# A gated attention decode kernel: the gate sum moved into the third projection's transposition, one signal for each query parity, the output sum copied in halves, the w2 products split

## The chip, the cores and the metric

The kernel runs on 1 core of one Trainium2 chip. The time is the device time of one execution in microseconds (us). A core has five engines that run programs of their own and meet at semaphores: TensorE (PE, matrix products), VectorE (DVE), ScalarE (ACT), GpSimd (POOL) and SyncE (SP, which here only issues DMAs).

## The reference

Two sequences, one token each, model width 448, 16 heads of 256, a cache of 4096 keys and values, and a dense block of 1792. All is float32.

```python
g = sigmoid((x * gate_w).sum(-1, keepdims=True))
q = (x @ wq).reshape(2, 1, 16, 256).transpose(0, 2, 1, 3)
p = softmax(einsum("bhqd,bhkd->bhqk", q, k_cache) * 256 ** -0.5)
a = einsum("bhqk,bhkd->bhqd", p, v_cache).reshape(2, 1, 4096) @ wo
b = relu(x @ w1) @ w2
out = g * a + (1 - g) * b
```

## The kernel before, in words

**The stream.** Every input is read once. There are U = 32 units, one for each pair of sequence and head. Row `kv[u]` (8 MB) holds the values of unit u and the keys of unit u+1. It lands in one of two slots of the ring in SBUF, `slot[u % 2]`. SP issues all large transfers in one hand-written order (L110 to L135): the two halves of wq, `kv[0]`, the keys of unit 0, the values of unit 1, w1, the keys of unit 2 (second half of `kv[1]`), then `kv[2]` to `kv[30]`, the values of unit 31, w2, and wo in six pieces of 13, 11, 4, 2, 1 and 1 chunks, the last ones the smallest. A transfer into a slot waits for `free`, which VectorE raises when it is done with the unit that lay there.

**A unit.** ScalarE copies the unit's query column out of `qt` into `query` (`pick`, L278). TensorE computes its scores with 16 matmuls (32 recorded passes, L192) into the one PSUM tile `ps`. VectorE takes the negative maximum (`peak`, L312), ScalarE the exponential with its sum (`exponents`, L283), and VectorE multiplies the 8 value blocks by the probabilities (`value`, L316). VectorE takes the next unit's maximum after its sixth value block. So while VectorE works on the values of u, TensorE does the scores of u+1. On ScalarE the order is: wait for the maximum, exponential, then `arrive` (L273: wait for the landing of `kv[u]`, raise `vals`), then `pick` of u+1, whose keys landed with it. VectorE waits for `prob` and `vals` before the values of u.

**The head.** POOL forms `gs`, the products of x and gate_w summed down to one number per partition; TensorE adds them over the partitions with a matmul of ones (L170), and ScalarE takes both sigmoids from it (L259, L260) and zeroes the PSUM tile `az` (L261). Then two projections with wq (L179), each copied to `wide` by ScalarE, transposed (L183) and copied to `qt`. The third projection, x @ w1, is done by TensorE once w1 has landed; ScalarE handles it in a branch in the middle of the loop, in its first turn after the second exponential (L292 to L302).

**The tail.** When w2 has landed, TensorE adds the 14 w2 chunks (28 passes, L226) into `acc`. After the last value block VectorE and ScalarE rescale the four partial softmaxes (L334 to L341), with two TensorE steps between (L231 into `wp`, L235 into `po`), and VectorE writes the gated attention output to `lhs` (L345, signal `ot`). Then TensorE adds 30 wo chunks (60 passes, L226), chunk groups as they land. The last two chunks go straight into `z` (L250). ScalarE copies `acc` to SBUF (L308), TensorE folds its four parts into `z` (L253), VectorE copies the result (L349), and SP writes it out.

**The branch hint.** TensorE's program is laid out in blocks. A never-taken branch at L244 back to the block `tail` carries a hint that is set at the very start (L168).

Of the kernel before, what the change touches and what calls it, by code (L numbers as in the profile page):

```python
# [9 lines left out]
G = 4  # L10
# [6 lines left out]
def take(e, sem, n=1):  # L17
    e.wait_ge(sem, n)
    e.sem_inc(sem, -n)  # L19
# [7 lines left out]
def gated_mix_decode(nc, xg, kv, wq, w1, w2, wo, out):  # L27
# [20 lines left out]
    NQ = H * DH // (G * CW)  # L48
    FG = NF * P // G
    WQ = wq.shape[2]  # L50
    SCALE = float(DH) ** -0.5
    assert NQ == 2 and U % 2 == 0 and U > 4 and FG == D and BL * GAP == NE * D and w1.shape[1] == WQ == BL * CW

    def sbuf(name, *shape):
        return nc.alloc_sbuf_tensor(name, [*shape], F32).ap()
# [5 lines left out]
    for n in (13, 11, 4, 2, 1, 1):  # L61
        WO.append(WO[-1] + n)
    assert WO[-1] == N
    names = ["xg", "wq", "w2", *(f"wo{k}" for k in WO[2:]), *(f"land{s}" for s in range(SLOTS)), "early",
             "pool", "vec", "act", "xr", "sums", "gate", "omg", "proj", "spent", "wide", "pt", "relu", "hr",
             "query", "score", "top", "prob", "vals", "free", "tr", "nb", "e4", "wb", "wp", "os", "po", "ot",
             "acc", "a", "z", "res", "out"]
    sem = {n: nc.alloc_semaphore(n) for n in names}
    land = [sem[f"land{s}"] for s in range(SLOTS)]

# [5 lines left out]
    ident = sbuf("ident", P, P)  # L76
    ones = sbuf("ones", P, P)
    sel2 = sbuf("sel2", P, HP)
    sel4 = sbuf("sel4", P, G, R)
    sel = sel4[:, 0]  # L80
    pg = sbuf("pg", P, B, KC)
    gs = sbuf("gs", P, B)
    gate = sbuf("gate", P, B)
    omg = sbuf("omg", P, B)
# [19 lines left out]
    acc, z = az[:, :D], az[:, CW:CW + DG]  # L104
    mt, lp, wp, gp = tp[:U, 0:P:R], tp[U:2 * U, 0:P:R], tp[:, 2 * P:2 * P + U], tp[:, 3 * P:3 * P + B]

# [35 lines left out]
    def gpsimd(e):  # L142
        settle(e, sem["pool"], e.memset(ident, 0.0))
        settle(e, sem["pool"], e.affine_select(out=ident, in_=ident, compare_op=ALU.not_equal, fill=1.0, base=0,
                                               pattern=[[-1, P]], channel_multiplier=1))
        e.memset(ones, 1.0)
        e.memset(qt[:, :, U:], 0.0)
        e.wait_ge(sem["xg"], 16)
        settle(e, sem["pool"], e.tensor_tensor(pg, xg_sb[:, :, :B].rearrange("p c b -> p b c"),
                                               xg_sb[:, None, :, B].to_broadcast([P, B, KC]), op=ALU.mult))  # L150
        settle(e, sem["pool"], e.memset(pg[HP:, :, KF:], 0.0))
        settle(e, sem["pool"], e.tensor_tensor(pg[:, :, :KC // 2], pg[:, :, :KC // 2], pg[:, :, KC // 2:], op=ALU.add))
        e.tensor_tensor(gs, pg[:, :, 0], pg[:, :, 1], op=ALU.add).then_inc(sem["sums"], 1)  # L153
        e.tensor_copy(xr.rearrange("p c (b r) -> p c b r", b=B),
                      xg_sb[:, :, :B, None].to_broadcast([P, KC, B, RB])).then_inc(sem["xr"], 1)
        settle(e, sem["pool"], e.tensor_tensor(sel2, ident[:, :HP], ident[:, HP:], op=ALU.add))
        e.tensor_tensor(sel4, sel2[:, None, :R].to_broadcast([P, G, R]), sel2[:, None, R:].to_broadcast([P, G, R]),
                        op=ALU.add)
        e.wait_ge(sem["omg"], 1)
        e.wait_ge(sem["relu"], 1)  # L160
        hid = lhs[:, :NF]
        settle(e, sem["pool"], e.tensor_tensor(hid, hid, omg[:, None, :].to_broadcast([P, NF, B]), op=ALU.mult))
        e.wait_ge(sem["w2"], 16)
        e.sem_inc(sem["hr"], 1)  # L164

    def tensor(e):
        outer = nc.cur_bb.parent
        stay = e.mark_branch_hint_location()  # L168
        e.wait_ge(sem["sums"], 1)
        e.matmul(gp, ones, gs, start=True, stop=True).then_inc(sem["gate"], 1)  # L170
        e.wait_ge(sem["xr"], 1)
# [13 lines left out]

        def scores(keys):
            take(e, sem["query"])
            for c in range(SG // CW):
                for t in range(T):
                    for g in range(G):  # L190
                        at = t * S + g * SG + c * CW
                        m = e.matmul(ps[g * R:(g + 1) * R, c * CW:(c + 1) * CW],  # L192
                                     query[:, t:t + 1].to_broadcast([P, R]), keys[:, at:at + CW], start=t == 0,
                                     stop=t == T - 1)
                        if c == SG // CW - 1 and t == T - 1:
                            m.then_inc(sem["score"], 1)
# [8 lines left out]
        for s in range(SLOTS):  # L205
            scores(slot[1 - s][:, VL:])
        e.br("next")
# [5 lines left out]
        nc.switch_bb("rest", parent=outer)  # L213
        e.wait_ge(sem["query"], 1)
        e.transpose(tp[:2 * U, :P], nl, ident).then_inc(sem["tr"], 1)  # L215
# [11 lines left out]

        for k in range(NF):
            add(k)
        e.wait_ge(sem["wb"], 1)  # L230
        e.transpose(wp, wb.rearrange("u g r -> u (g r)"), ident[:U, :U]).then_inc(sem["wp"], 1)  # L231
        e.br("tail")
        nc.switch_bb("tail", parent=outer)
        e.wait_ge(sem["os"], 1)
        e.matmul(po[:, :G * nu], sel4.rearrange("p g r -> p (g r)"), os.rearrange("p u j -> p (u j)"), start=True,  # L235
                 stop=True).then_inc(sem["po"], 1)
        for k in range(NF, N - DIRECT):
            if k == NF:
                e.wait_ge(sem["ot"], 17)
            elif k in WO:  # L240
                e.wait_ge(sem[f"wo{WO[WO.index(k) + 1]}"], 16)
            m = add(k)
        m.then_inc(sem["acc"], 1)
        e.br_lt(turn, 0, on_true="tail", on_false="fold").branch_hint(stay)  # L244
        nc.switch_bb("fold", parent=outer)
        for k in range(N - DIRECT, N):
            e.wait_ge(sem[f"wo{k + 1}"], 16)
            for g in range(G):
                lo = (k - NF) * D + g * DG
                e.matmul(z[g * R:g * R + B], lhs[:, k], slot[0][:, lo:lo + DG], start=k == N - DIRECT, stop=False)  # L250
        e.wait_ge(sem["a"], 1)
        for g in range(G):
            m = e.matmul(z[g * R:g * R + B], sel[:, :B], a_sb[:, g * DG:(g + 1) * DG], start=False, stop=True)  # L253
        m.then_inc(sem["z"], 1)

    def scalar(e):
        bring(e, xg_sb, xg, sem["xg"])
        e.wait_ge(sem["gate"], 1)
        e.activation(omg, gp, AF.Sigmoid, scale=-1.0).then_inc(sem["omg"], 1)  # L259
        e.activation(gate, gp, AF.Sigmoid)  # L260
        e.activation(az, qt[:, 0, U:].to_broadcast([P, 2 * CW]), AF.Copy)  # L261
        for i in range(NQ):
# [7 lines left out]
                         pt.rearrange("p (s t n r) -> p s t n r", s=2, t=T, r=RB)[:, :, :, :, 0],  # L270
                         AF.Copy)

        def arrive(s):  # L273
            take(e, land[s], 16)
            e.sem_inc(sem["vals"], 1)

        def pick(u):
            e.activation(query, qt[:, :, bass.ds(u, 1)].rearrange("p t o -> p (t o)"), AF.Copy).then_inc(  # L278
                sem["query"], 1)

        def exponents(u, s):
            take(e, sem["top"])
            e.activation(prob[:, s * SG:(s + 1) * SG], ps, AF.Exp, bias=nm[:, bass.ds(u, 1)],  # L283
                         accum_out=ls[:, bass.ds(u, 1)]).then_inc(sem["prob"], 1)

        take(e, land[1], 16)
        pick(0)
        with e.Fori(0, U // 2) as i:
            for s in range(SLOTS):
                exponents(i * 2 + s, s)  # L290
                if s:
                    with e.If(i < 1):  # L292
                        take(e, sem["proj"])
                        e.activation(wide[:, :FG], ph[:, :FG], AF.Copy).then_inc(sem["wide"], 1)
                        take(e, sem["pt"])
                        e.activation(lhs[:, :G * KF],
                                     pt[:, :KF * P].rearrange("p (k b r) -> p k b r", b=B, r=RB)[:, :, :, 0], AF.Relu)
                        for h in range(2):
                            half = pt[:HP, KF * P + h * HP:KF * P + (h + 1) * HP]
                            m = e.activation(lhs[h * HP:(h + 1) * HP, G * KF:NF],  # L300
                                             half.rearrange("p (k b r) -> p k b r", b=B, r=RB)[:, :, :, 0], AF.Relu)
                        m.then_inc(sem["relu"], 1)  # L302
                arrive(s)
                pick(i * 2 + (s + 1))
        e.wait_ge(sem["nb"], 1)
        e.activation(e4, mt, AF.Exp, bias=nb, scale=-1.0).then_inc(sem["e4"], 1)
        e.wait_ge(sem["acc"], 1)
        e.activation(a_sb, acc, AF.Copy).then_inc(sem["a"], 1)  # L308

    def vector(e):  # L310
# [3 lines left out]
        def value(u, j, at, half):  # L314
            v = ring[:, bass.ds(at + j * SG, SG)]
            return e.scalar_tensor_tensor(v, v, 1.0, prob[:, bass.ds(half, SG)], op0=ALU.mult, op1=ALU.mult,  # L316
                                          accum_out=ov[:, bass.ds(u, 1), j])

        take(e, sem["score"], G)
        e.sem_inc(sem["free"], 1)  # L320
        peak(0)
        e.wait_ge(sem["early"], 16)
        with e.Fori(0, U) as u:
            take(e, sem["prob"])
            take(e, sem["vals"])
            for j in range(J):
# [87 lines left out]
```

## Time and profile before

| | |
|---|---|
| time, median of 3 runs | 675.07 us (674.78 to 675.76) |
| the profiled execution's own time | 674.93 us |
| its span, first to last instruction | 673.3 us |
| read from HBM | 289.54 MB |
| mean rate over the span | 430 GB/s |
| VectorE busy | 334.7 us (50%) |
| TensorE busy | 218.1 us (32%) |
| ScalarE busy | 71.4 us (11%) |

How to read it: the span lies 1.6 us under the time of the same execution; the rest is start and end around the first and last instruction. Timeline rows give start, duration, engine, line, operation, tile written and read, shape, and in brackets how long the engine had been idle and who released it. `x4` means four merged instructions, so the duration of a merged row covers all of them. A float32 matmul is recorded as two passes. PEld is the weight load of a matmul, PEclk the granted TensorE clock as a share of full.

### The profile page before, as it was taken

How to read it: one execution, taken by the hardware profiler on the slowest of the kernel's cores; microseconds unless marked ns; L12 is line 12 of the kernel's file. 1: busy time of each engine (PE TensorE's matmuls, PEld its weight loads, DVE VectorE, ACT ScalarE, POOL GpSimd, SP SyncE). 2: the span in 40 equal slices, each digit the busy share in tenths (PEclk: the TensorE clock that was granted, in tenths of full speed). 3: DMA queues.
4: the chain of work that ended last, by engine and by line, in shares of the span. 5: the costliest groups of instructions: out<-in, count | busy, mean ns of one | idle time of the engine just before them, and what ended most of it. 6: DMA issues, size and time to landing. Idle time of an engine off the chain costs nothing. (4 is left out here: it accounts for less than half of the span.)

```text
span 673.3 us, 4293 instructions
## 1 busy us (share of the span) xinstructions
PE 218.1 (32%) x1250; PEld 55.0 (8%) x1250; DVE 334.7 (50%) x556; ACT 71.4 (11%) x127; POOL 2.8 (0%) x16
## 2 busy tenths in 40 slices
PE   2146522233333212333331133333212333332247
PEld 0011100000000000000000000000000000000001
DVE  0005544566654445666444456654444666544491
ACT  1001110101001010101001010100101010010100
POOL 1000000000000000000000000000000000000000
PEclk9766766776765567676556767766556766655678
DMA  9999999999999999999999999999999999999997
GB/s 405 414 427 436 467 436 436 436 424 436 432 409 432 432 428 432 436 436 436 436 436 436 436 436 436 436 436 436 436 436 436 436 436 436 436 436 436 405 429 331
DMA packets 6625, 289.62 MB, mean 430 GB/s; under 512 B 992, under 2 KB 1248, under 8 KB 1504
## 3 DMA queue, kind: packets, MB, share of 16 engines
q1 hardware_dynamic: 6480, 289.60, 99.4%
q10 hardware_dynamic: 144, 0.01, 0.0%
q8 instruction: 1, 0.02, 0.0%
HBM read 289.54 MB, written 0.06 MB: 430 GB/s over the span
## 5 line engine op out<-in xcount | busy, mean ns | idle before, releaser
L316 DVE SCALAR_TENSOR_TENSOR ring<-ring,prob x256 | 297.9, 1220 | 269.8 <-DVEq L19 269.8
L192 PE MATMUL ps<-ring,query 128*32 128x512 f32 x1024 | 184.0, 884 | 405.2 <-PEq L19 405.2
L192 PEld LDWEIGHTS ps<-ring,query 128*32 128x32 f32 x1024 | 46.5, 154 | 541.4 <-issue 541.4
L312 DVE TENSOR_REDUCE nl<-ps 128x1024 f32 (+1 forms) x32 | 39.0, 1220 | 55.3 <-DVEq L19 55.3
L283 ACT ACTIVATE prob<-ps,nl 128x1024 f32<-128x1024 f32 x32 | 35.6, 1113 | 134.8 <-ACTq L19 134.6
L283 ACT ACT_TABLE_LOAD x16 | 20.5, 1283 | 132.9 <-ACTq L19 132.9
L278 ACT ACTIVATE query<-qt 128x2 f32 (+1 forms) x33 | 6.7, 204 | 262.9 <-ACTq L19 262.9
L179 PE MATMUL ph<-weights,xr 128*32 128x512 f32 (+1 forms) x96 | 15.0, 767 | 20.7 <-DMA weights<-in_wq 19.0
L316 DVE DVE_READ_ACCUMULATOR ring<-ring,prob x256 | 21.0, 82 | 0.0
L226 PE MATMUL az<-ring,lhs 128*2 128x448 f32 x60 | 8.8, 664 | 1.1 <-DVE lhs L345 1.0
L226 PE MATMUL az<-weights,lhs 128*2 128x448 f32 x28 | 5.7, 908 | 5.6 <-POOLq L164 5.6
L283 ACT ACTIVATION_READ_ACCUMULATOR prob<-ps,nl x32 | 6.2, 192 | 0.0
L179 PEld LDWEIGHTS ph<-weights,xr 128*32 128x32 f32 (+1 forms) x96 | 3.0, 133 | 31.2 <-DMA weights<-in_wq 19.2
L349 DVE COPY res<-az 128x112 f32<-128x112 f32 x1 | 0.3, 274 | 9.9 <-PE az L253 9.9
L170 PE MATMUL tp<-gs,ones 128*128 128x2 f32 x2 | 0.6, 364 | 13.3 <-POOL gs L153 13.3
L265 ACT ACTIVATE wide<-ph 128x512 f32<-128x512 f32 x2 | 1.2, 597 | 28.9 <-ACTq L19 28.9
L183 PE MATMUL pt<-ident,wide 128*128 128x128 f32 x12 | 2.0, 287 | 2.5 <-ACT wide L265 1.8
L226 PEld LDWEIGHTS az<-ring,lhs 128*2 128x2 f32 x60 | 1.8, 95 | 7.6 <-issue 4.1
L308 ACT ACTIVATE wide<-az 128x448 f32<-128x448 f32 x1 | 0.5, 543 | 12.6 <-PE az L226 12.6
L226 PEld LDWEIGHTS az<-weights,lhs 128*2 128x2 f32 x28 | 1.0, 114 | 9.4 <-POOLq L164 5.8
L183 PEld LDWEIGHTS pt<-ident,wide 128*128 128x128 f32 x12 | 1.3, 141 | 5.2 <-ACT wide L265 3.6
L215 PE MATMUL tp<-ident,nl 128*64 128x128 f32 x1 | 0.3, 299 | 4.3 <-ACT query L278 4.3
(43 smaller groups left out, 13.5 us busy)
## 6 DMA issues: line engine op xcount, KB each, us to landing
ring<-in_kv SPq DMA_DIRECT2D x4, 4096.0 KB, 24.8
weights<-in_wq SPq DMA_DIRECT2D x2, 3584.0 KB, 14.8
weights<-in_w SPq DMA_DIRECT2D x1, 3584.0 KB, 20.0
ring<-in_wo SPq DMA_DIRECT2D x1, 2912.0 KB, 12.0
weights<-in_w SPq DMA_DIRECT2D x1, 2688.0 KB, 23.9
ring<-in_wo SPq DMA_DIRECT2D x1, 2464.0 KB, 17.4
ring<-in_wo SPq DMA_DIRECT2D x1, 896.0 KB, 19.0
ring<-in_kv SPq DMA_DIRECT2D x30, 27.5
```

Of the source, the lines that this page charges most:

```text
L170: e.matmul(gp, ones, gs, start=True, stop=True).then_inc(sem["gate"], 1)
L179: m = e.matmul(ph[g * R:(g + 1) * R], xr[r, c], weights[r, at:at + CW], start=c == 0, stop=c == KC - 1)
L183: t = e.transpose(pt[:, k * P:(k + 1) * P], wide[:, k * P:(k + 1) * P], ident)
L192: m = e.matmul(ps[g * R:(g + 1) * R, c * CW:(c + 1) * CW], query[:, t:t + 1].to_broadcast([P, R]), keys[:, at:at + CW], start=t == 0, stop ...
L215: e.transpose(tp[:2 * U, :P], nl, ident).then_inc(sem["tr"], 1)
L226: return e.matmul(acc[g * R:g * R + B], lhs[:, k], w, start=k < G, stop=k >= N - DIRECT - G)
L265: e.activation(wide, ph, AF.Copy, scale=SCALE).then_inc(sem["wide"], 1)
L278: e.activation(query, qt[:, :, bass.ds(u, 1)].rearrange("p t o -> p (t o)"), AF.Copy).then_inc(sem["query"], 1)
L283: e.activation(prob[:, s * SG:(s + 1) * SG], ps, AF.Exp, bias=nm[:, bass.ds(u, 1)], accum_out=ls[:, bass.ds(u, 1)]).then_inc(sem["prob"], 1)
L308: e.activation(a_sb, acc, AF.Copy).then_inc(sem["a"], 1)
L312: e.tensor_reduce(nm[:, bass.ds(u, 1)], ps, axis=AX.X, op=ALU.max, negate=True).then_inc(sem["top"], 1)
L316: return e.scalar_tensor_tensor(v, v, 1.0, prob[:, bass.ds(half, SG)], op0=ALU.mult, op1=ALU.mult, accum_out=ov[:, bass.ds(u, 1), j])
```

## The change

- **Gate.** The matmul of ones, its two sigmoids and the `ones` tile go. POOL writes `gs`, repeated 32 times for each sequence, into the 64 columns of `wide` that the third projection leaves free (after both wq rounds: `spare`, then `column`). The third projection's transposition, which covered those columns already, turns them into rows; ScalarE copies these 64 rows with a sum over the free dimension (`gl`), POOL spreads the sums to the partitions with 8 small copies (`gp`), ScalarE takes one sigmoid in the branch of the first turn, and POOL forms 1 - gate.
- **Zeroing.** `az` is zeroed by VectorE at its start instead of by ScalarE.
- **Query signals.** `query` becomes `query0` and `query1`. TensorE only waits for one; ScalarE lowers it again before the exponential. TensorE's program loses two instructions by it.
- **Landing.** `arrive` and `vals` go. `exponents` now first waits for the landing of `kv[u]`, then for the maximum. VectorE waits for `prob` alone.
- **Tail.** The w2 products are split 8, 2 and 4 chunks: the step into `wp` comes after the first 8, the step into `po` after the next 2. The blocks `tail` and `fold` with their branches and the hint go. `acc` is copied in two halves of 224 columns, and each fold matmul waits for its half.

```diff
-        e.memset(ones, 1.0)
...
-        e.tensor_tensor(gs, pg[:, :, 0], pg[:, :, 1], op=ALU.add).then_inc(sem["sums"], 1)
+        settle(e, sem["pool"], e.tensor_tensor(gs, pg[:, :, 0], pg[:, :, 1], op=ALU.add))
...
-        e.wait_ge(sem["omg"], 1)
-        e.wait_ge(sem["relu"], 1)
+        e.wait_ge(sem["spare"], NQ)
+        e.tensor_copy(wide[:, FG:].rearrange("p (b r) -> p b r", b=B),
+                      gs[:, :, None].to_broadcast([P, B, R])).then_inc(sem["column"], 1)
+        e.wait_ge(sem["logit"], 1)
+        for g in range(G):
+            for b in range(B):
+                m = e.tensor_copy(gp[g * R:(g + 1) * R, b:b + 1], gl[HP + b * R:HP + (b + 1) * R, :1])
+        m.then_inc(sem["gate"], 1)
+        e.wait_ge(sem["sigmoid"], 1)
+        settle(e, sem["pool"], e.tensor_scalar(omg, gate, -1.0, 1.0, op0=ALU.mult, op1=ALU.add))
...
-        stay = e.mark_branch_hint_location()
-        e.wait_ge(sem["sums"], 1)
-        e.matmul(gp, ones, gs, start=True, stop=True).then_inc(sem["gate"], 1)
...
-        def scores(keys):
-            take(e, sem["query"])
+        def scores(s):
+            keys = slot[1 - s][:, VL:]
+            e.wait_ge(query_set[s], 1)
...
-        for k in range(NF):
+        for k in range(NF - 6):
             add(k)
         e.wait_ge(sem["wb"], 1)
         e.transpose(wp, wb.rearrange("u g r -> u (g r)"), ident[:U, :U]).then_inc(sem["wp"], 1)
-        e.br("tail")
-        nc.switch_bb("tail", parent=outer)
+        for k in range(NF - 6, NF - 4):
+            add(k)
         e.wait_ge(sem["os"], 1)
...
-        for k in range(NF, N - DIRECT):
+        for k in range(NF - 4, N - DIRECT):
...
-        e.br_lt(turn, 0, on_true="tail", on_false="fold").branch_hint(stay)
-        nc.switch_bb("fold", parent=outer)
...
-        e.wait_ge(sem["a"], 1)
         for g in range(G):
+            e.wait_ge(sem["a"], 1 + g * DG // HALF)
             m = e.matmul(z[g * R:g * R + B], sel[:, :B], a_sb[:, g * DG:(g + 1) * DG], start=False, stop=True)
...
-        e.wait_ge(sem["gate"], 1)
-        e.activation(omg, gp, AF.Sigmoid, scale=-1.0).then_inc(sem["omg"], 1)
-        e.activation(gate, gp, AF.Sigmoid)
-        e.activation(az, qt[:, 0, U:].to_broadcast([P, 2 * CW]), AF.Copy)
...
-        def arrive(s):
-            take(e, land[s], 16)
-            e.sem_inc(sem["vals"], 1)
...
         def exponents(u, s):
+            take(e, land[s], 16)
             take(e, sem["top"])
+            e.sem_inc(query_set[s], -1)
             e.activation(prob[:, s * SG:(s + 1) * SG], ps, AF.Exp, bias=nm[:, bass.ds(u, 1)],
                          accum_out=ls[:, bass.ds(u, 1)]).then_inc(sem["prob"], 1)
...
                     with e.If(i < 1):
                         take(e, sem["proj"])
+                        e.wait_ge(sem["column"], 1)
                         e.activation(wide[:, :FG], ph[:, :FG], AF.Copy).then_inc(sem["wide"], 1)
                         take(e, sem["pt"])
+                        e.activation(gl[HP:, 1:], pt[HP:, KF * P:], AF.Copy, accum_out=gl[HP:, :1]).then_inc(
+                            sem["logit"], 1)
...
-                        m.then_inc(sem["relu"], 1)
-                arrive(s)
-                pick(i * 2 + (s + 1))
+                        e.wait_ge(sem["gate"], 1)
+                        e.activation(gate, gp, AF.Sigmoid).then_inc(sem["sigmoid"], 1)
+                pick(i * 2 + (s + 1), 1 - s)
...
-        e.activation(a_sb, acc, AF.Copy).then_inc(sem["a"], 1)
+        for lo in range(0, D, HALF):
+            e.activation(a_sb[:, lo:lo + HALF], acc[:, lo:lo + HALF], AF.Copy).then_inc(sem["a"], 1)
...
+        e.memset(az, 0.0)
         take(e, sem["score"], G)
...
             take(e, sem["prob"])
-            take(e, sem["vals"])
```

More of the change, by code (lines that the diff above doesn't have):

```diff
@@ L49, in gated_mix_decode @@
     FG = NF * P // G
+    HALF = D // 2
     WQ = wq.shape[2]
@@ L64, in gated_mix_decode @@
     names = ["xg", "wq", "w2", *(f"wo{k}" for k in WO[2:]), *(f"land{s}" for s in range(SLOTS)), "early",
-             "pool", "vec", "act", "xr", "sums", "gate", "omg", "proj", "spent", "wide", "pt", "relu", "hr",
-             "query", "score", "top", "prob", "vals", "free", "tr", "nb", "e4", "wb", "wp", "os", "po", "ot",
+             "pool", "vec", "act", "xr", "spare", "column", "logit", "gate", "sigmoid", "proj", "spent", "wide", "pt", "hr",
+             "query0", "query1", "score", "top", "prob", "free", "tr", "nb", "e4", "wb", "wp", "os", "po", "ot",
              "acc", "a", "z", "res", "out"]
     sem = {n: nc.alloc_semaphore(n) for n in names}
+    query_set = [sem[f"query{s}"] for s in range(2)]
     land = [sem[f"land{s}"] for s in range(SLOTS)]
@@ L76, in gated_mix_decode @@
     ident = sbuf("ident", P, P)
-    ones = sbuf("ones", P, P)
     sel2 = sbuf("sel2", P, HP)
@@ L82, in gated_mix_decode @@
     gs = sbuf("gs", P, B)
+    gl = sbuf("gl", P, 1 + P)
+    gp = sbuf("gp", P, B)
     gate = sbuf("gate", P, B)
@@ L104, in gated_mix_decode @@
     acc, z = az[:, :D], az[:, CW:CW + DG]
-    mt, lp, wp, gp = tp[:U, 0:P:R], tp[U:2 * U, 0:P:R], tp[:, 2 * P:2 * P + U], tp[:, 3 * P:3 * P + B]
+    mt, lp, wp = tp[:U, 0:P:R], tp[U:2 * U, 0:P:R], tp[:, 2 * P:2 * P + U]
     def bring(e, dst, src, signal):
@@ L205, in tensor @@
         for s in range(SLOTS):
-            scores(slot[1 - s][:, VL:])
+            scores(s)
         e.br("next")
@@ L213, in tensor @@
         nc.switch_bb("rest", parent=outer)
-        e.wait_ge(sem["query"], 1)
+        e.wait_ge(query_set[0], 1)
         e.transpose(tp[:2 * U, :P], nl, ident).then_inc(sem["tr"], 1)
@@ L270, in scalar, with pick, exponents @@
                          pt.rearrange("p (s t n r) -> p s t n r", s=2, t=T, r=RB)[:, :, :, :, 0],
-                         AF.Copy)
-        def arrive(s):
-            take(e, land[s], 16)
-            e.sem_inc(sem["vals"], 1)
[L277 to L281, printed above, removed]
+                         AF.Copy).then_inc(sem["spare"], 1)
+        def pick(u, s):
+            e.activation(query, qt[:, :, bass.ds(u, 1)].rearrange("p t o -> p (t o)"), AF.Copy).then_inc(
+                query_set[s], 1)
+        def exponents(u, s):
+            take(e, land[s], 16)
             take(e, sem["top"])
+            e.sem_inc(query_set[s], -1)
             e.activation(prob[:, s * SG:(s + 1) * SG], ps, AF.Exp, bias=nm[:, bass.ds(u, 1)],
@@ L286, in scalar @@
         take(e, land[1], 16)
-        pick(0)
+        pick(0, 0)
         with e.Fori(0, U // 2) as i:
@@ L299, in scalar @@
                             half = pt[:HP, KF * P + h * HP:KF * P + (h + 1) * HP]
-                            m = e.activation(lhs[h * HP:(h + 1) * HP, G * KF:NF],
+                            e.activation(lhs[h * HP:(h + 1) * HP, G * KF:NF],
                                              half.rearrange("p (k b r) -> p k b r", b=B, r=RB)[:, :, :, 0], AF.Relu)
-                        m.then_inc(sem["relu"], 1)
-                arrive(s)
-                pick(i * 2 + (s + 1))
+                        e.wait_ge(sem["gate"], 1)
+                        e.activation(gate, gp, AF.Sigmoid).then_inc(sem["sigmoid"], 1)
+                pick(i * 2 + (s + 1), 1 - s)
         e.wait_ge(sem["nb"], 1)
```

## The prediction

> **What bounds the kernel now.** First the page: the span, the row of DMA shares, the instruction queue.
>
> ```profile
> span 673.3 us, 4293 instructions
> ...
> DMA  9999999999999999999999999999999999999997
> ...
> q8 instruction: 1, 0.02, 0.0%
> HBM read 289.54 MB, written 0.06 MB: 430 GB/s over the span
> ```
>
> The DMA engines are busy nine tenths or more in 39 of 40 slices, and 289.54 MB at 430 GB/s are the whole span. No engine can shorten that stream; it can only be interrupted, or the end behind its last byte can change. So I read the end next, in the chain that ended last.
>
> ```profile
> 650.65 19.90 DMA ring<-in_wo
> ...
> 670.60 0.37 PE az L250 x8
> 670.97 0.02 issue
> 670.99 0.42 PE az L253 x8
> ```
>
> The last wo piece lands at 670.55, and 2.7 us later the program ends. Two questions follow: does the changed kernel keep the queue full, and is everything but the last chunk done by 670.55? For both I read the timeline of the end.
>
> ```profile
> 637.64 0.20 ACT L278 ACTIVATE query<-qt 128x2 f32 x1 [8.23 <-ACTq L19]
> 637.91 1.22 DVE L316 SCALAR_TENSOR_TENSOR ring<-ring,prob  x1 [8.92 <-DVEq L19]
> ...
> 648.38 2.71 SPq L108 DMA_DIRECT2D ring<-in_wo  x6
> ...
> 653.48 5.66 PE L226 MATMUL az<-weights,lhs 128*2 128x448 f32 x28 [5.60 <-POOLq L164]
> ...
> 657.38 0.14 DVE L334 TENSOR_REDUCE nb<-tp 32x1 f32<-32x4 f32 x1
> ...
> 658.46 0.28 DVE L339 TENSOR_SCALAR wb<-e,rl 32x128 f32<-32x128 f32 x1
> ...
> 659.07 0.24 PE L231 MATMUL tp<-ident,wb 32*128 32x32 f32 x1
> ...
> 659.83 0.70 PE L235 MATMUL po<-os,sel 128*128 128x256 f32 x2 [0.51 <-DVE os L341]
> ...
> 661.54 8.81 PE L226 MATMUL az<-ring,lhs 128*2 128x448 f32 x60 [1.01 <-DVE lhs L345]
> ...
> 662.63 0.16 PEld L226 LDWEIGHTS az<-ring,lhs 128*2 128x2 f32 x4 [0.58 <-issue]
> 663.38 0.17 PEld L226 LDWEIGHTS az<-ring,lhs 128*2 128x2 f32 x4 [0.58 <-issue]
> ...
> 666.21 0.12 PEld L226 LDWEIGHTS az<-ring,lhs 128*2 128x2 f32 x8 [0.63 <-DMA ring<-in_wo]
> ...
> 669.43 0.09 PEld L226 LDWEIGHTS az<-ring,lhs 128*2 128x2 f32 x4 [0.86 <-DMA ring<-in_wo]
> ...
> 670.40 0.54 ACT L308 ACTIVATE wide<-az 128x448 f32<-128x448 f32 x1 [12.58 <-PE az L226]
> ```
>
> `kv[30]` has landed by 637.64. From 637.91 VectorE works without a gap to 657.4, then come the softmax steps, and TensorE starts the 60 wo passes at 661.54. It overtakes the stream: 0.63 us idle at 666.21, 0.86 at 669.43. So before the end there is slack, but little: the path from the landing of `kv[30]` through VectorE to TensorE is the second longest thing in the kernel. The stages show VectorE full and the clock that TensorE got:
>
> ```profile
> 646.00:653.40 7.40, 0.30 (x1) 0.11 (x1) 7.40 (x14) 1.30 (x3) 0.00 (x0) 0.65 1.00 429
> ...
> 658.50:661.90 3.40, 1.88 (x11) 0.54 (x11) 1.53 (x6) 0.00 (x0) 0.00 (x0) 1.00 1.08 463
> 661.90:665.30 3.40, 3.40 (x24) 0.75 (x17) 0.00 (x0) 0.00 (x0) 0.00 (x0) 0.51 0.91 393
> 665.40:670.00 4.60, 4.56 (x40) 0.94 (x35) 0.00 (x0) 0.00 (x0) 0.00 (x0) 1.00 0.96 391
> ```
>
> Four passes take 0.75 us at half clock (662.63 to 663.38), 0.1875 each, so 0.094 at full clock; the clock turned full about 665.4.
>
> **The change, part by part.** *Landing before exponential.* This is the part that moves most. Today the exponential runs as soon as the maximum is there, some 8 us before the landing; then only `pick` waits. Now the exponential itself stands behind the landing, and `pick` and VectorE's values behind the exponential. Its price from the first unit:
>
> ```profile
> 56.79 1.28 ACT L283 ACT_TABLE_LOAD   x1 [7.25 <-ACTq L19]
> 58.08 1.11 ACT L283 ACTIVATE prob<-ps,nl 128x1024 f32<-128x1024 f32 x1
> 59.09 0.19 ACT L283 ACTIVATION_READ_ACCUMULATOR prob<-ps,nl  x1
> ...
> 59.84 1.23 DVE L316 SCALAR_TENSOR_TENSOR ring<-ring,prob  x1 [3.28 <-DVEq L19]
> ```
>
> Exponential and accumulator read take 1.20 us (58.08 to 59.28). If the exponential of unit 30 starts where `pick` starts now, 637.64, `prob` is up at 638.84. VectorE follows 0.27 later (as 637.91 follows 637.64) to 0.56 later (59.28 to 59.84): 639.11 to 639.40, a delay of 1.20 to 1.49; I take 1.35. In the middle of the stream this is covered by the next transfer, already queued. At the end: wo is issued at 649.7 instead of 648.38, and w2 ahead of it is still arriving until 653.48, so the queue keeps over 3 us of work. But VectorE has no gap left, so the whole chain from 657.38 moves by 1.35: `wb` ends at 660.09 instead of 658.74.
>
> *Where the tables are loaded.* The trace has 16 loads at L283, one in two units, always ahead of the even exponential: the loop is entered with the sigmoid's tables, so its first exponential must load. After the change the sigmoid sits in a branch inside the loop; a load in every turn must stay, since the program cannot know whether the branch ran. It can stand ahead of the even exponential as now (then unit 30 starts 1.28 later still) or, nearer to the branch, ahead of the `pick` behind it, where only the next scores are late. At the loop's entry nothing needs a sigmoid any more, which speaks for the second; I take it, and keep 1.28 us for a rival.
>
> *w2 in three parts.* 28 passes in 5.66 us are 0.20 each. The first 16 end at 656.7, so `wp` no longer stands behind them: it starts 0.05 after `wb`, 660.14, instead of 0.33 after it. From `wp` to `po` are 0.76 us now, so `po` could start at 660.90; the two chunks between (4 passes, 0.8 us, after `wp`'s 0.24) hold it to 661.2. `po` to the first wo pass is 1.71 us now: 662.9. The last four chunks (8 passes, 1.6 us at half clock) come first and end between 663.1 and 663.5, as they may start before or after the end of `po`'s 0.70. So the wo passes start at 663.3, 1.76 us later than today. Until 665.4 that is 11 passes, and the other 49 take 4.6 us: 670.0. No piece of wo holds them. Today the last four start at 669.43 and end at 669.81. **Cost 0.2 us**, straight on the path, because `acc` is what the 670.40 copy waits for.
>
> *Copy in halves.* 448 columns take 0.54 us. Two halves take at least that together and at most twice it; being pipelined I take 0.60, with the first two fold groups started earlier. The fold today starts 0.02 after L250's end at 670.97, so nothing can be gained beyond 0.1; the last group may be later by the second fixed cost. Between -0.1 and +0.3; I take **+0.05**.
>
> *Gate sum in the third transposition.* It takes TensorE's first matmul and ScalarE's head work away, ahead of a projection whose next step waits for transfers: nothing. What is added lies in the first turn, while the stream runs from its queue:
>
> ```profile
> 1.86 0.10 POOL L147 MEMSET qt<- 128x2 f32 x1
> ...
> 13.17 0.29 POOL L154 COPY xr<-xg_sb 128x128 f32<-128x128 f32 x1
> ...
> 71.35 0.54 ACT L294 ACTIVATE wide<-ph 128x448 f32<-128x448 f32 x1 [1.98 <-ACTq L19]
> ...
> 72.73 0.19 ACT L296 ACTIVATE lhs<-pt 128x24 f32<-128x24 f32 x1 [0.83 <-ACTq L19]
> ```
>
> ```profile
> 77.31 0.20 ACT L278 ACTIVATE query<-qt 128x2 f32 x1 [4.16 <-ACTq L19]
> ...
> 77.66 5.61 PE L192 MATMUL ps<-ring,query 128*32 128x512 f32 x32 [5.05 <-PEq L19]
> ...
> 84.46 1.22 DVE L312 TENSOR_REDUCE nl<-ps 128x1024 f32 x1
> ...
> 88.20 19.67 SPq L108 DMA_DIRECT2D ring<-in_kv  x2
> 96.64 0.20 ACT L278 ACTIVATE query<-qt 128x2 f32 x1 [8.25 <-ACTq L19]
> ```
>
> The branch now runs behind unit 1's exponential, which waits for the landing at 77.31. Exponential 1.11, copy to transposed rows 1.38 (71.35 to 72.73), the summing copy and its read about 0.5 (a 24-column copy is 0.19), 8 small POOL copies 0.8 to 2.3 (0.10 for the small set, 0.29 for the large copy; nearest to the small: 1.0), sigmoid with its load partly beside the copies 0.7, reload 1.28: `pick` of unit 2 at 83.3, 6.0 us late. Queued behind it on ScalarE is only that `pick`; TensorE waits for it, VectorE for TensorE. Scores end at 83.7 + 5.6 = 89.3, so the maximum of 84.46 comes 4.8 late and the next `kv` issue moves from 88.2 to 93.0. The transfer ahead of it lands by 96.64: 3.6 us of cover. Cost nothing; if the cover went, each further us would be lost one for one.
>
> [...]
>
> *Query signals, branches, hint, zeroing.* TensorE waits for data behind each of these instructions; nothing.
>
> **The sum.** 0.2 + 0.05 on the profiled execution's 674.93 is 675.2. That execution lies 0.14 under the median of 675.07, so the forecast on the median is **675.3 us**. About 0.2% (1.35 us) is what a measurement of this kernel can tell from no change; this is within it.
>
> **The rivals.**
>
> *TensorE's wo passes become the bound (slower).* Place: from 663.3 to the `acc` copy. It decides when the passes end after 669.81. If the table load stays ahead of the even exponential, they start at 664.6 and end 0.64 later than forecast: 675.9. If the clock turns full one stage of 3.4 us later, 18 passes more run at half clock: 1.7 us later, 677.0. For it: TensorE now idles from 656.7 to 660.1, and only a stage filled 3.40 of 3.40 brought the full clock, while the one filled 1.88 of 3.40 was followed by half. [...] Against it: at today's phase the turn at 665.4 still fits. Chance 0.22, half of it over 676.4.
>
> *The stream runs dry in the first turn (slower).* If the POOL copies and table switches take 3 us more than I add up, the 3.6 us less a transfer's own start are gone, and up to 1.5 us of all engines are lost: up to 676.8. Against it: the rows above. Chance 0.08.
>
> *The program is not short enough.* The one instruction packet of 0.02 MB would fall into the stream: 0.02 MB at a sixteenth of 430 GB/s holds one engine for 0.7 us, 676.0. [...] Chance 0.05.
>
> *A slightly shorter end.* The passes are not late at all and half of `acc` is folded early: -0.1 to -0.2, 674.9. Chance 0.10.
>
> **How the numbers follow.** The forecast keeps 0.55. Slower by over 0.2%: 0.11 of the first rival, 0.05 of the second, 0.01 of the rest: 0.17. Faster by over 0.2% would need half of the 2.7 us behind the last byte, and no part touches that much: 0.03. Same: 0.80. The range goes from 674.7 (short end, with the spread of the runs) to 676.9, which leaves out the worst clock phase.
>
> **What would show it.** Right: the values of unit 30 start 1.2 to 1.5 us behind `pick`'s old place, at about 639.3; the wo passes start near 663.3 with no idle time at the second piece; the 16 loads stand at the query copy, not at the exponential; the instruction packet is gone. Wrong: a DMA share under nine tenths near 95 us; a fold that starts over 1 us later than 670.99, or a span shorter by over 1 us.

## The result and the profile after

The changed kernel takes 681.93 us (median of 6 runs, 680.75 to 683.37), the kernel before 675.44 us beside it (6 runs). The ratio is 1.01, its interval 1.0086 to 1.0113: slower by 6.5 us, and outside the range that was forecast. The profiled execution of the changed kernel took 682.86 us, with a span of 681.4.

The page of the changed kernel: the DMA shares in 40 slices of 17 us, their rates, and two groups (line, engine, operation, count, then busy time and mean ns): the 16 table loads, which now stand at the query copy, and the new copies.

```profile
DMA  9999979999999999999999999999999999999997
GB/s 400 410 434 435 442 308 396 446 442 439 431 435 431 431 431 431 431 431 431 431 431 431 431 431 431 431 431 431 458 442 450 435 431 431 431 431 431 414 432 304
...
L276 ACT ACT_TABLE_LOAD x16 | 20.5, 1283 | 0.3
...
L167 POOL COPY gp<-gl 32x1 f32<-32x1 f32 x8 | 5.5, 692 | 33.6 <-ACT gl L297 33.4
```

One slice of the stream is no longer full: the sixth, 85 to 102 us, at 308 GB/s. The stages there and SyncE's issue say where (columns: stage, its length, busy time and count of PE, PEld, DVE, ACT and POOL, clock, DMA share, GB/s; a DMA packet is counted whole in the stage where it starts):

```profile
90.00:95.00 5.00, 5.00 (x24) 1.07 (x28) 0.00 (x0) 0.00 (x0) 0.00 (x0) 0.50 1.00 433
95.00:101.20 6.20, 2.95 (x20) 0.60 (x16) 4.36 (x6) 1.30 (x3) 0.00 (x0) 0.78 0.00 0
```

```profile
100.58 0.34 SPq L111 DMA_DIRECT2D ring<-in_kv  x1
```

The 0 GB/s say that no packet starts between 95.00 and 101.20; those under way, of 2.42 us each, still run out. By the trace's packets fifteen of the 16 DMA engines end their last one between 95.62 and 96.48 us and the sixteenth at 97.47, and the next ones start from 101.56 on, 0.98 after the issue at 100.58. So each engine is empty for 5.7 us in the mean, and for 4.1 us all are. In the kernel before the same issue stood at 88.20. The timeline ahead of it:

```profile
82.25 5.83 POOL L167 COPY gp<-gl 32x1 f32<-32x1 f32 x8 [33.36 <-ACT gl L297]
...
82.71 1.22 DVE L320 SCALAR_TENSOR_TENSOR ring<-ring,prob  x1
...
88.11 0.20 ACT L306 ACTIVATE gate<-gp 128x2 f32<-128x2 f32 x1 [4.19 <-POOL gp L167]
88.33 1.28 ACT L276 ACT_TABLE_LOAD   x1
...
89.62 0.20 ACT L276 ACTIVATE query<-qt 128x2 f32 x1
```

The eight GpSimd copies of one column take 5.83 us; behind them stand the sigmoid, a table load, the query of unit 2, its scores, VectorE's maximum and the last two value blocks of unit 1, and behind those the issue. The second place is the end. Its chain no longer begins with a transfer:

```profile
666.99 0.29 DVE wb L343
667.28 0.04 issue
667.32 0.31 PE tp L239
667.64 1.59 PE az L234 x4
669.22 1.15 PE po L243 x2
670.38 7.39 PE az L234 x65
677.77 0.29 PE az L256 x7
```

From the softmax weights on, TensorE bounds the end; before, it waited there for wo. A third difference stands in no group. The instruction packet of 16 KB (queue q8), at 670.5 us in the trace before, starts at 25.8 us in this one. From then until the empty stretch one of the 16 DMA engines lands behind the others: `kv[0]` between 30.59 and 31.47 on fifteen of them and at 32.52 on the last, where before all sixteen landed between 30.54 and 31.07.

### The profile page after: what moved, and what is told of

It is laid out like the page before. It is cut to its first block, busy times and chain, and to the rows that moved or that the text cites. A ratio compares the mean times of both kernels' runs of the same rounds, so it can differ in the third digit from the quotient of the medians.

```text
span 681.4 us, 4236 instructions
## 1 busy us (share of the span) xinstructions
PE 217.7 (32%) x1248; PEld 49.3 (7%) x1248; DVE 336.4 (49%) x557; ACT 70.6 (10%) x129; POOL 8.7 (1%) x25
## 5 line engine op out<-in xcount | busy, mean ns | idle before, releaser
L200 PEld LDWEIGHTS ps<-ring,query 128*32 128x32 f32 x1024 | 40.6, 155 | 542.8 <-ACT query L276 431.2
L234 PE MATMUL az<-ring,lhs 128*2 128x448 f32 x60 | 6.7, 574 | 0.0
L167 POOL COPY gp<-gl 32x1 f32<-32x1 f32 x8 | 5.5, 692 | 33.6 <-ACT gl L297 33.4
```

What stands on the lines that cost most here:

```text
L167: m = e.tensor_copy(gp[g * R:(g + 1) * R, b:b + 1], gl[HP + b * R:HP + (b + 1) * R, :1])
L200: m = e.matmul(ps[g * R:(g + 1) * R, c * CW:(c + 1) * CW], query[:, t:t + 1].to_broadcast([P, R]), keys[:, at:at + CW], start=t == 0, stop ...
L234: return e.matmul(acc[g * R:g * R + B], lhs[:, k], w, start=k < G, stop=k >= N - DIRECT - G)
```

## The experiments

Three theories were held against each other. S: the GpSimd copies in the first turn delay a `kv` issue until the stream runs dry. T: the end is late, by the exponential behind the landing and by the order of the w2 products. P: without the branch hint (and the branch and blocks that went with it) the instruction packet falls into the stream. Differences below are to the kernel before in the same comparison.

**e1: the sigmoid behind the loop.**

```diff
 (in the first turn)
-                        e.wait_ge(sem["gate"], 1)
-                        e.activation(gate, gp, AF.Sigmoid).then_inc(sem["sigmoid"], 1)
 (after the loop)
+        e.wait_ge(sem["gate"], 1)
+        e.activation(gate, gp, AF.Sigmoid).then_inc(sem["sigmoid"], 1)
         e.wait_ge(sem["nb"], 1)
```

> The changed kernel, with the wait for the gate sums and the sigmoid moved from the loop's first turn to behind the loop. Theory S (the 8 GpSimd copies, held by VectorE, stand ahead of the third query and let the stream run dry at 95 to 101 us): the query copy of unit 2 comes at about 82.7 us instead of 89.6, the fourth kv issue before 94, no empty stretch, and the time falls to about 677.5 (what is left over 675.4 is the late last wo passes and the early instruction packet). Rival (the exponential behind the landing alone empties the stream): the stretch stays several us long and the time is over 680. The copies themselves stay as slow, 0.8 us in the mean. The table loads in every turn should go, since the loop holds no sigmoid any more.

Measured: 677.34 us (7 runs) against 675.31, ratio 1.0028 (1.0017 to 1.004). The query of unit 2 is copied at 82.61. SyncE's row:

```profile
93.31 0.34 SPq L111 DMA_DIRECT2D ring<-in_kv  x1
```

The empty stretch is gone (0.3 us per engine in the mean are left of 5.7) and 4.5 of the 6.5 us with it, although the exponential still stands behind the landing. So what empties the stream is what ScalarE does ahead of the query because of the sigmoid: the wait for the copies, the sigmoid itself and the table load behind it, 7.0 us together (89.62 to 82.61). The copies themselves stayed as slow (836 ns in the median, 838 in the changed kernel), and the table load in every second unit is gone, as expected: three loads are left in the whole trace.

**e2: the copies by ScalarE.**

```diff
-                m = e.tensor_copy(gp[g * R:(g + 1) * R, b:b + 1], gl[HP + b * R:HP + (b + 1) * R, :1])
+                m = e.activation(gp[g * R:(g + 1) * R, b:b + 1], gl[HP + b * R:HP + (b + 1) * R, :1], AF.Copy)
```

> The changed kernel with the 8 small copies done by ScalarE instead of GpSimd, at the same place. Theory S: they take about 1.2 us instead of 5.8, the query copy of unit 2 comes at about 86.3, the fourth kv issue at about 97, so the empty stretch shrinks from 5.7 to about 2 us and the time to about 678.5 to 679.5. Rival (copies don't matter, the branch as such is too long): the empty stretch keeps over 4 us, time over 681.

Measured: 679.17 us (4 runs) against 675.31, ratio 1.0061 (1.0045 to 1.0078), within what S expected. The row of the copies (ns min/median/max, first and last start) and SyncE's:

```profile
L303 ACT ACTIVATE gp<-gl x8: 198/200/201, 82.5 to 83.9; 32x1 f32<-32x1 f32 x8
```

```profile
96.86 0.34 SPq L111 DMA_DIRECT2D ring<-in_kv  x1
```

The issue comes 3.7 us earlier. The way from the exponential to the query copy is 2.45 us shorter of it (78.57 to 86.96, against 78.78 to 89.62); most of the rest is scores that took 5.53 us instead of 6.59. That is not enough: the engines run out from about 95.5 on, as in the changed kernel, and stay empty for 2.1 us in the mean. So the slow copies are the larger part of the stretch, not all of it; in this run the sigmoid's table load also stands behind the copies, no longer beside them.

**e3: the old landing order.**

```diff
         def exponents(u, s):
-            take(e, land[s], 16)
             take(e, sem["top"])
...
+                take(e, land[s], 16)
+                e.sem_inc(sem["vals"], 1)
                 pick(i * 2 + (s + 1), 1 - s)
...
             take(e, sem["prob"])
+            take(e, sem["vals"])
```

> The changed kernel with the old order on ScalarE: exponential when the maximum is there, then the wait for the landing and the signal for VectorE. Theory S: the copies then run while VectorE waits (70 to 77 us), take about 0.2 each, and the whole branch ends before the landing at 78: no empty stretch. The values of unit 30 start 0.5 us after its landing instead of 2.0, so the wo passes start about 1.4 us earlier against the stream than in the changed kernel. Time about 676.5 to 677: what is left is the early packet (about 1) and the order of the w2 products. Rival (the end of the kernel or the signals cost the time): over 679.

Measured: 676.21 us (10 runs) against 675.31, ratio 1.0015 (1.0005 to 1.0024), 0.3 us under the lower edge of what was expected. This run also says why the copies are slow. In the changed kernel the copies run while VectorE multiplies values, here while it still waits for the landing. First the changed kernel's row, then two of e3's timeline, then its copies:

```profile
L167 POOL COPY gp<-gl x8: 180/838/1108, 82.3 to 87.9; 32x1 f32<-32x1 f32 x8
```

```profile
77.44 1.72 POOL L167 COPY gp<-gl 32x1 f32<-32x1 f32 x8 [28.96 <-ACT gl L296]
...
79.72 1.23 DVE L321 SCALAR_TENSOR_TENSOR ring<-ring,prob  x1 [8.28 <-DVEq L19]
79.87 1.17 POOL L172 TENSOR_TENSOR lhs<-lhs,omg 128x28 f32<-128x28 f32 x1 [0.18 <-POOLq L19]
```

```profile
L167 POOL COPY gp<-gl x8: 176/179/184, 77.4 to 79.0; 32x1 f32<-32x1 f32 x8
```

The same copies take 179 ns each with VectorE idle. And the product at L172, 0.23 us in the kernel before, takes 1.17 here, because VectorE's first value product began at 79.72. In the changed kernel the first copy begins in the middle of a value product, the next four take 1.10 to 1.11 us each, and all five end 0.04 us behind the end of a product (the first at 82.83 behind 82.78, the fifth at 87.41 behind 87.37). The last three, after VectorE had stopped to wait for scores, are 0.18 again. So of GpSimd's instructions that met VectorE's value products in these two traces, one got through at the end of each product.

**e4: the branch hint back.**

```diff
+        stay = e.mark_branch_hint_location()
...
+        e.br("tail")
+        nc.switch_bb("tail", parent=outer)
         for k in range(NF - 6, NF - 4):
...
+        e.br_lt(turn, 0, on_true="tail", on_false="fold").branch_hint(stay)
+        nc.switch_bb("fold", parent=outer)
```

> The changed kernel with the branch hint and the two blocks back, all else kept. Theory P (the instruction packet at 25.8 us comes because the hint is gone, and one DMA engine then lands about 1.2 us behind the others): the packet moves to the end, the landings of one transfer spread over 0.6 us again instead of 1.9 until 97 us; the stream still runs dry for about 5.5 us, and the time falls by 0.5 to 1.4 us. Rival: the packet has nothing to do with the hint and stays at 25.8 us, time unchanged at 681.9.

Measured: 680.70 us (4 runs) against 675.31, ratio 1.0082 (1.0066 to 1.0099): 1.1 us less over the kernel before than the changed kernel. The packet is at 675.4 us, behind the stream. The landings of `kv[0]` spread over 1.1 us, not the 0.6 expected, but none stands apart (the last two at 31.53 and 31.69). The stretch is still there, but not the 5.5 us expected: 3.6 us in the mean of the engines.

```profile
98.36 0.34 SPq L111 DMA_DIRECT2D ring<-in_kv  x1
```

With the packet away, the landing that starts the branch comes earlier, and the exponential with it by 0.74 us (78.04 instead of 78.78). The issue is 2.2 us earlier; most of the other 1.5 us are scores that took 5.11 us instead of 6.59, since the granted clock turned full at 92.2 us (at 95.9 in the changed kernel). The 1.1 us are thus not the packet's alone, and the intervals of this kernel and the changed one overlap.

**e5: the kernel before without the hint.** The edit of e4 in reverse, on the kernel before.

> The kernel before, with the branch hint, its never-taken branch and the two blocks taken out, nothing else. Theory P: the 16 KB instruction packet falls into the stream near 26 us, one DMA engine lands about 1.3 us behind the others from then to the end, and since no empty stretch absorbs it the last wo piece lands at about 671.8 instead of 670.55: time about 676.4. Rival: the packet is harmless, or stays at the end: 675.3.

Measured: 676.61 us (11 runs) against 675.17, ratio 1.0024 (1.0015 to 1.0033). The packet is at 25.9 us, and the last wo piece lands at 669.98 on the first engine and at 671.85 on the last one (669.93 and 670.55 before). A second packet follows at 676.0 us, behind the last instruction. The early packet and the 1.3 us by which the last landing is late account for the 1.4 us: P holds. The hint, its branch and the two blocks went together, here and in e4; which of the three holds the packet back is not shown.

**e6: landing order and hint both back.** The edits of e3 and e4 together.

> The changed kernel with both the old landing order and the hint back; gate sum in the transposition, query signals, w2 in three parts and the halved copy remain. If landing order and packet are all that costs time: 675.2 to 675.4, no different from before, packet near 670 us, landings spread over 0.6 us. If the w2 order or the halves cost something by themselves: 675.7 to 676.5.

Measured: 675.15 us (11 runs) against 675.17, ratio 0.9999 (0.999 to 1.0008). Gate sum, query signals, w2 in three parts and halved copy are all still in it: together with the old landing order they cost and bring nothing that can be told. The packet is at 671.0 us; the landings of `kv[0]` spread over 1.0 us instead of the 0.6 expected.

**e7: sigmoid behind the loop, hint back.** The edits of e1 and e4 together.

> The changed kernel with the sigmoid behind the loop and the hint back. No empty stretch and no early packet, so what is left is the end: the values of unit 30 start 2.0 us after its landing, the wo passes about 2.7 us later than before. Expected 676.0 to 676.6. If the late end is hidden by the stream: 675.3.

Measured: 676.55 us (11 runs, 675.25 to 677.36) against 675.17, ratio 1.0017 (1.0008 to 1.0026). What is left, 1.4 us (0.5 to 1.8 by the interval), is the end. Next to e6, which differs in the landing order and the place of the sigmoid, the values of unit 30 start 1.25 us later (639.54 instead of 638.29) and the first wo weights 1.29 us later (664.52 instead of 663.23). So the first half of T, the exponential behind the landing, holds.

**e8: the same with w2 whole.**

```diff
-        for k in range(NF - 6):
+        for k in range(NF):
             add(k)
...
-        for k in range(NF - 6, NF - 4):
-            add(k)
...
-        for k in range(NF - 4, N - DIRECT):
+        for k in range(NF, N - DIRECT):
```

> The same with the 14 w2 chunks in one piece ahead of the softmax steps, as before. Theory: the split costs about 1.3 us of the late start, because the step into po waits until the two chunks ahead of it have drained and the last four stand ahead of wo; so the wo passes start at about 662.8 and the time is 675.3 to 675.7, below the run with the split. Rival: the late VectorE chain alone makes the end late: as slow as with the split, over 676.

Measured: 675.87 us (11 runs) against 675.17, ratio 1.0014 (1.0005 to 1.0023), 0.2 us over what was expected. The second half of T, the w2 order, is not shown by the time: the medians of e7 and e8 are 0.7 us apart, but their means only 0.2, and their runs cover the same range (675.25 to 677.36 and 675.61 to 677.03). The traces say why. TensorE's rows, e7 first:

```profile
660.45 0.31 PE L240 MATMUL tp<-ident,wb 32*128 32x32 f32 x1 [3.61 <-DVE wb L348]
660.69 1.66 PE L235 MATMUL az<-weights,lhs 128*2 128x448 f32 x4
662.28 1.22 PE L246 MATMUL po<-os,sel 128*128 128x256 f32 x2
663.43 1.67 PE L235 MATMUL az<-weights,lhs 128*2 128x448 f32 x8
664.88 5.85 PE L235 MATMUL az<-ring,lhs 128*2 128x448 f32 x58
```

```profile
660.66 0.25 PE L240 MATMUL tp<-ident,wb 32*128 32x32 f32 x1 [0.72 <-DVE wb L346]
661.42 0.70 PE L244 MATMUL po<-os,sel 128*128 128x256 f32 x2 [0.51 <-DVE os L348]
663.13 7.50 PE L235 MATMUL az<-ring,lhs 128*2 128x448 f32 x58 [1.01 <-DVE lhs L352]
```

With w2 whole the step into `po` stands 0.76 us behind the step into `wp`; with the split 1.83, because it starts only when the four passes ahead of it are done, and itself takes 1.22 instead of 0.70. The wo passes start 1.75 us later. But the same 58 of them then take 5.85 us instead of 7.50. The granted clock (the third number from the end) differs, in e7 first:

```profile
660.40:663.40 3.00, 2.95 (x7) 0.78 (x7) 0.42 (x1) 0.00 (x0) 0.00 (x0) 0.50 1.02 440
663.40:665.00 1.60, 1.60 (x13) 0.32 (x16) 0.88 (x4) 0.00 (x0) 0.00 (x0) 0.51 1.09 468
665.00:666.60 1.60, 1.60 (x24) 0.40 (x20) 0.00 (x0) 0.00 (x0) 0.00 (x0) 1.00 0.84 355
```

```profile
660.40:663.40 3.00, 1.22 (x7) 0.54 (x11) 1.50 (x6) 0.00 (x0) 0.00 (x0) 0.96 1.04 447
663.40:665.00 1.60, 1.60 (x12) 0.32 (x8) 0.00 (x0) 0.00 (x0) 0.00 (x0) 0.50 1.00 431
665.00:666.60 1.60, 1.60 (x12) 0.32 (x8) 0.00 (x0) 0.00 (x0) 0.00 (x0) 0.50 0.82 346
```

With the split TensorE goes through the softmax steps at half clock and gets the full clock from 665 us on, in time for the wo passes; with w2 whole it is the other way round, and the wo passes run at half clock until 666.6. The copies of `acc` start only 0.11 us apart (671.16 and 671.05). What the w2 order costs in other executions, with the clock turning at another time, stays open.

**e9, e10, e11: a shorter TensorE program.** They ask whether the packet's time hangs on the program's length. On e3; 16, 40 and 136 instructions of TensorE less, by leaving chunks out of the sum:

```diff
         def add(k):
+            if k in range(10, 14):
+                return None
```

(`range(4, 14)` in e10, `range(4, 38)` in e11.)

> The changed kernel with the old landing order (so that nothing else disturbs the stream) and the last four w2 chunks left out of the sum: TensorE's program is 16 instructions shorter still. [...]

> The same with ten w2 chunks left out, 40 instructions. [...]

> The same with ten w2 and 24 wo chunks left out, 136 instructions: the program is then well over a quarter shorter. [...]

One execution each. The packet stays, at 25.7, 28.1 and 28.2 us, with one engine behind as in e3. So it does not hang on the program's length, as far as 136 instructions reach; in all traces with the hint the first packet came behind the stream, in all without at 25.7 to 28.3 us. Their times (676.05, 676.24 and 677.98 us) belong to less work and are not compared.

## Why the prediction was wrong

A ladder of medians divides the 6.5 us: the end 1.38 (e7 over before), the empty stretch another 4.01 (e4 is 5.39 over before), the packet another 1.10 (the changed kernel is 6.49 over). The last step is the least certain, and there the packet acts through the stretch: it delays the landing that the branch waits for (without it the exponential comes 0.74 us earlier, e4), while its own lag is gone behind the stretch.

**The step that failed** is the sum for the first turn, "8 small POOL copies 0.8 to 2.3 (0.10 for the small set, 0.29 for the large copy; nearest to the small: 1.0)". Measured were 5.83 us, over twice the upper end. The rows that I took for the bounds were from the first 14 us, in which VectorE does nothing; the copies in the branch run beside VectorE's value products. The profile before did not show GpSimd and VectorE at work together anywhere: GpSimd's one late instruction, at 73.30, also fell between the products. The range should have had the length of a value product, 1.2 us, as its upper end: 8 of these are 10 us, and they would have made the rival the forecast. e3 shows the difference: 179 ns each beside an idle VectorE, against 1.10 to 1.11 us for four of the changed kernel's copies beside its value products.

**What went with it.** The rival of the stream running dry had the right mechanism and place, but a chance of 0.08 and a price of at most 1.5 us. Its cover, "3.6 us", was read from the time at which ScalarE saw the landing. The engines run out from 95.6 on, and the transfer there started to move 0.98 us behind its issue, so an issue after about 94.6 leaves engines empty: 1.6 us from the forecast 93.0. The other 2.8 us of delay from 93.0 to 100.58 that the copies do not explain (4.8 of 7.6) are mostly the exponential that begins the branch, 1.47 late (78.78 instead of 77.31; in e4, without the early packet, 78.04), and scores at half clock, 6.59 us instead of the 5.61 that I took. The rest are small: the maximum follows the end of the scores by 0.4 us (96.47 to 96.84), which I left out. These 2.8 us alone would have used up the cover; the copies made a gap of it that cost 4 us.

**Hint and program length** were put at "nothing", with the rival "the program is not short enough" at 0.05 and 0.7 us. The packet does fall into the stream; it costs 0.9 us in e3 (over e6) and 1.4 in e5. But the rival's reason is not borne out: leaving out 136 instructions more doesn't remove it (e11). That the program's length decides when the packet comes was my assumption; no run shows it.

**The end** was put at 0.25 us and measured 1.4. Right were the first steps: VectorE's values 1.62 us behind the start of the exponential (in the changed kernel 644.80 to 646.44, 1.64), the 16 table loads at the query copy, the next step 0.05 after `wb`, and 0.60 us for the two halves. Wrong was w2: the four passes between `wp` and `po` were put at 0.8 us and hold `po` for 1.6 (667.64 to 669.22 in the chain above), `po` was kept at today's 0.70 and took 1.22. I counted what passes add to a running row of passes; here the step that waited for the row to end waited for its last pass too. The same slip is in today's end: the row of 60 ends at 670.35 (661.54 and 8.81), just ahead of the `acc` copy at 670.40, not at the 669.81 that I read. And `po` ran at half clock, as in e7 above, behind a TensorE that had idled for 3.6 us ahead of `wp` (0.72 in e8, where `po` got the full clock). From the exponential to the first wo passes are 26.6 us in the changed kernel (644.80 to 671.39, where its first wo weights are loaded), against 25.7 forecast. The rival of TensorE as the bound had this place, at 0.22. Of the 1.4 us the exponential behind the landing is shown as a cause (e7 beside e6); the w2 order is not, beyond the later start.

## What to carry to other kernels

A small GpSimd instruction beside VectorE's value products cost up to a whole product here, 1.1 us instead of 0.18; take its duration only from a row where the two run together, and otherwise bound it by one VectorE instruction each. In a kernel bound by one saturated stream, follow every chain that ends in the next issue, and measure its slack from the end of the packets, not from the wait that sees the landing. Taking out the hint with its branch and blocks brought the 16 KB instruction packet into the stream here (at 25.8 us instead of 670.5), and one of the 16 DMA engines that carry the stream then landed 1.05 us behind the next-latest (32.52 against 31.47).

## What the runs showed of the hardware

One 16 KB packet, 0.93 to 0.94 us long, put one of 16 DMA engines 1.0 to 1.4 us behind the next-latest, and in the unbroken stream of e5 that engine stayed behind to the end, some 645 us later (the packet at 25.9, the last landing at 671.85, against 670.55 in the kernel before). The empty stretch took that lag away: in the changed kernel the landings after 101 us lie within 0.7 us of each other again. Open stays what the packet holds, what of the hint, the branch and the blocks keeps it out, and why its time moves between 25.7 and 28.3 us.
